# Feed-forward blocks of 512 tokens, with the last 64 tokens of every batch gathered into a ninth block, in a fused attention, Fourier-mixing and feed-forward kernel

## The chip, the cores and the metric

The kernel runs on one core of a Trainium2 chip. The metric is the device time of one execution in microseconds (us), as the median of several runs. TensorE (PE) multiplies, VectorE (DVE), ScalarE (ACT) and GpSimd (POOL) work on elements, and the queue of SyncE (SP) issues nearly all transfers.

## What is computed

The reference, cut to what matters:

```python
# attention: batch 8, heads 8, seq 576, head_dim 64; keys and values averaged in groups of 8 (72 remain)
scores = scale * np.matmul(q, k_p.transpose(0, 1, 3, 2))
attn = softmax(scores)
x = np.matmul(attn, v_p)              # -> (8, 576, 512)
# mixing: the real part of a 2-D Fourier transform over tokens and channels of one batch
u = x + np.real(np.fft.fft(np.fft.fft(x, axis=1), axis=2))
un = (u - mean(u)) / np.sqrt(var(u) + 1e-06)
out = u + np.maximum(un @ w_ch1, 0.0) @ w_ch2   # 512 -> 2048 -> 512
```

All is float32. Each large product is made from three products of rounded numbers (high by high, low by high, high by low).

## The kernel before

A generator `fe(b)` (L247) is the front end of one batch of 576 tokens, and `ffn` (L705) is the feed-forward part of one block of tokens. The program is written as one loop over blocks (L815): each `ffn` yields twice per step, and at each yield (a position, `pos`) `advance` (L790) lets the front ends of later batches take their next stage, and `prep_w` (L178) prepares one of the 34 pieces of the weights where `need(pos)` (L811) asks for it. A scheduler then fixes the order of the instructions of each engine; the engines work through their queues in that order.

**The feed-forward part.** A block of `nb` tokens goes through 16 steps `f` of 128 hidden channels. A step is 12 matmuls into a PSUM tile `g1` (L731: four channel groups times three products, with the centred input as a high part `unh` and a low part `unl`, and the weights as `w1h` and `w1low`), the positive part split into `hh` (ACT, L735) and `hl` (DVE, L736), and 12 matmuls into four PSUM tiles `acc` (L715, with `w2h` and `w2low`), which come one step later. So a step has 24 matmuls, each as wide as the block. After the last step DVE multiplies each `acc` by the tokens' scale `rb` (L745) and adds it to `U` (L746), and SP stores `U` (L748). The low parts of the weights lie in DRAM (`wls`, L92) and are read again at each step (`load_low`, L211) into a ring of seven places (tag `w`).

**The blocks** (`blocks`, L71). Batch 0 goes in halves of 288 tokens, first both halves through steps 0 to 7 and then both through 8 to 15; batches 1 to 6 go in pairs, each pair of 1152 tokens in three blocks of 384; batch 7 goes in two halves of 288. There are 208 steps in all, 64 of 288 columns and 144 of 384.

**The front end of a batch.** For each of four pairs of heads: loads of keys, queries and values, scores (`psS`, L345), softmax, transposes (`psT`, L385), values (`psX`, L432) into the one tile `X`. Then the channel transform (`psA` L547, `psB` L575), whose results are split on ACT and DVE into `A`, `B` and `AB` (L529 to L535), and the token transform (`psQ`, `psP`, L592). This last stage ends so, from batch 2 on: DVE adds `psQ` and `psP` to `U` and `X` (L598, L599, L607, L608); POOL forms sums and differences in four instructions (L624, L625), while DVE, ACT and DVE again make the sum over channels (`s`, L617 to L620); PE averages it (`psM`, L642, L643); DVE subtracts the mean (L644); ACT rounds `unh` in four instructions (L632); DVE and POOL make `unl`, two instructions each (L633). The scale `rb` follows some stages later. Each batch has a slot of 576 columns in `unh`, `unl`, `U` and `rb` (`slot`, L67), even batches the second and odd ones the first; `free` (L753) gives the position from which the next user of a slot may write it. A front end writes `X` only when the one before it has left it, and the products of the front end share two PSUM tiles (tag `fe`).

Of the kernel before, what the change touches and what calls it, by code (L numbers as in the profile page):

```python
# [8 lines left out]
F32 = mybir.dt.float32  # L9
F32R = mybir.dt.float32r  # L10
# [36 lines left out]
UE = [4, 1, 0]  # L47
UL = [3, 3, 2]

AHEAD, LEAD, PACE = 11, 12, 0.65  # L50

THIRD = 18

# [1 line left out]
E0, O0, E1, O1 = 0, 1, 2, 3  # L55
# [23 lines left out]
def raw(ap):  # L79
    return ap.bitcast(F32)  # L80
# [3 lines left out]
def tile_kernel(ctx: ExitStack, tc: tile.TileContext, qt, kt, vm, vr, w1, w2, cad, cbd, mkd, out):  # L84
    nc = tc.nc
    cp = ctx.enter_context(tc.tile_pool(name="cp", bufs=1))
    wk = ctx.enter_context(tc.tile_pool(name="wk", bufs=1))
# [24 lines left out]
    U = cp.tile([P, 4, RING], F32, name="U")  # L112
# [103 lines left out]
    steps = [f for *_, f0, f1 in blocks() for f in range(f0, f1)]  # L216


    turn, behind = [0], {}
# [27 lines left out]
    def fe(b):  # L247
# [6 lines left out]
        def load(g):  # L254

            k = U[:, g, 0:S] if b == 0 else wk.tile([P, S], F32, tag="k", name=f"k{b}_{g}")
            nc.sync.dma_start(k, kt[b, g])
            q = U[:, g, S:RING] if b == 0 else wk.tile([P, S], F32, tag="q", bufs=2, name=f"q{b}_{g}")
            nc.sync.dma_start(q, qt[b, g])
            st["q", g], st["k", g] = q, k.rearrange("p (j w) -> p j w", w=POOLW)  # L260
# [4 lines left out]
            st["v", g] = v.rearrange("p (d w) -> p d w", d=D)  # L265

        def load_rem(gi):
            r = wk.tile([32, D, POOLW], F32, tag="vr", name=f"vr{b}_{gi}")
            nc.sync.dma_start(r, vr[b, gi].rearrange("p (d w) -> p d w", d=D))
            st["r", gi] = r  # L270

        def total(out, src, pool):

# [428 lines left out]

    at = [0]

    def ffn(ro, nb, to, f0, f1):  # L705
        cl = slice(ro, ro + nb)
        acc = [pp.tile([P, 512], F32, tag=f"acc{e}", name=f"acc{to}_{f0}_{e}")[:, 0:nb] for e in range(4)]

        def gemm2(f, hh, hl, wh, wl):
            order = [(x, e) for x in range(3) for e in range(4)]  # L710
            if f == f1 - 1:
                order = [(x, e) for e in range(4) for x in range(3)]
            for x, e in order:
                w, h = ((wh, hh), (wl, hh), (wh, hl))[x]
                nc.tensor.matmul(acc[e], lhsT=w[:, e], rhs=h, start=(f == f0 and x == 0), stop=(f == f1 - 1 and x == 2))  # L715

        prev = None
        for f in range(f0, f1):
# [8 lines left out]
            ps = pp.tile([P, 512], F32, tag="g1", bufs=2, name=f"g1_{to}_{f}")[:, 0:nb]  # L727
            n = 0
            for w, x in ((ah, unh), (ah, unl), (al, unh)):
                for c, ti in enumerate((E0, O0, E1, O1)):  # L730
                    nc.tensor.matmul(ps, lhsT=w[:, c], rhs=x[:, ti, cl], start=(n == 0), stop=(n == 11))  # L731
                    n += 1
            hh = wk.tile([P, 384], F32R, tag="hh", bufs=2, name="hh")[:, 0:nb]
            hl = wk.tile([P, 384], F32R, tag="hl", bufs=2, name="hl")[:, 0:nb]
# [7 lines left out]
        gemm2(f1 - 1, *prev)  # L742
        for e in range(4):
            u = U[:, e, cl]
            nc.vector.tensor_tensor(out=acc[e], in0=acc[e], in1=rb[:, cl], op=ALU.mult)  # L745
            nc.vector.tensor_tensor(out=u, in0=u, in1=acc[e], op=ALU.add)  # L746
# [4 lines left out]
    free = {1: 0, 2: 64, 3: 128, 4: 160, 5: 224, 6: 256, 7: 320}  # L753
# [36 lines left out]
    def advance(pos):  # L790
        for b in sorted(run):
            r = run[b]
            if r[3] is None:

                upto = (pos + 1 - r[2]) * (npre / (free[b] - 1) if b == 2 else 1)
            else:
                upto = r[3] + pos - max(free[b], r[2]) + 1 if pos >= free[b] else 0
            while r[1] < upto:
                said = next(r[0], "end")
                r[1] += 1  # L800
                if said == "U":
# [12 lines left out]
    pos = 0
    for blk in blocks():  # L815
# [116 lines left out]
```

## Time and profile before

| what | value |
|---|---|
| median of 3 runs | 1094.45 us (1093.58 to 1095.3) |
| span of the profiled execution (the page gives no other time of it) | 1094.2 us |
| PE busy | 1050.1 us, 96% |
| DVE, ACT, POOL busy | 611.6, 416.0, 247.3 us |
| feed-forward matmuls (6 groups of 832) | 4992 |
| loads of low weights (2 groups of 208, 256 KB each) | 416 |
| moved by DMA | 175.80 MB |

How to read it: "busy" is time in which an instruction of the engine was running. Matmuls overlap, and the profile models their ends, so the cost of a matmul is read from the distance between starts and not from its duration. A row of the timeline has the start, the time until the last of the merged instructions ends, the engine, the line, the operation, out<-in and the count. PEclk is the share of full clock that PE was granted. The page's 40 slices show PE at nine tenths or more from the tenth slice on, and lower before.

### The profile page before, as it was taken

How to read it: one execution, taken by the hardware profiler on the slowest of the kernel's cores; microseconds unless marked ns; L12 is line 12 of the kernel's file. 1: busy time of each engine (PE TensorE's matmuls, PEld its weight loads, DVE VectorE, ACT ScalarE, POOL GpSimd, SP SyncE). 2: the span in 40 equal slices, each digit the busy share in tenths (PEclk: the TensorE clock that was granted, in tenths of full speed). 3: DMA queues.
4: the chain of work that ended last, by engine and by line, in shares of the span. 5: the costliest groups of instructions: out<-in, count | busy, mean ns of one | idle time of the engine just before them, and what ended most of it. 6: DMA issues, size and time to landing. Idle time of an engine off the chain costs nothing.

```text
span 1094.2 us, 17702 instructions
## 1 busy us (share of the span) xinstructions
PE 1050.1 (96%) x6606; PEld 1017.7 (93%) x6606; DVE 611.6 (56%) x1237; ACT 416.0 (38%) x1102; POOL 247.3 (23%) x249
## 2 busy tenths in 40 slices
PE   8848898999999999999999999999999999999997
PEld 7637887999999999999999999999999999999997
DVE  7686878856376455756377455756467434522222
ACT  6767764443143331443233341443324322311110
POOL 4463356212230032201240121400322101200000
PEclk9968999999999999999999999999999999999999
DMA  7867977565345454445444444445534334346563
GB/s 242 274 204 254 318 250 227 178 199 170 119 122 161 121 162 135 127 140 166 131 120 148 142 151 130 133 125 156 158 108 155 98 98 124 117 128 189 165 186 99
DMA packets 91878, 175.80 MB, mean 161 GB/s; under 512 B 10128, under 2 KB 17296, under 8 KB 91536
## 3 DMA queue, kind: packets, MB, share of 16 engines
q1 hardware_dynamic: 91504, 172.01, 50.7%
q0 software_dynamic: 288, 2.66, 0.7%
q8 instruction: 52, 0.85, 0.3%
q14 instruction: 34, 0.28, 0.1%
HBM read 156.81 MB, written 17.83 MB: 160 GB/s over the span
## 4 chain that ended last, share of the span: by engine, by line
PE 84%; DVE 6%; DMA 4%; ACT 3%; issue 1%; POOL 1%; SPq 0%; DVEq 0%; POOLq 0%; ACTq 0%
PE acc L715 35%; PE g L731 35%; PE psX L432 3%; PE psS L345 3%; PE psA L547 2%; PE psP L592 2%; DMA wst<-in_w 1%; DMA w1low<-w1l 1%; PE psB L575 1%; PE psT L385 1%; DVE wd L199 1%; PE psQ L592 1%; DVE wd L198 1%; DMA k<-in_kt 1%; PE psR L408 1%
## 5 line engine op out<-in xcount | busy, mean ns | idle before, releaser
L735 ACT ACTIVATE hh<-g 128x384 fp32r<-128x384 f32 (+1 forms) x208 | 96.3, 464 | 309.6 <-PE g L731 289.8
L736 DVE SCALAR_TENSOR_TENSOR hl<-g,hh 128x384 fp32r<-128x384 f32 (+1 forms) x208 | 108.6, 522 | 185.0 <-ACT hh L735 183.2
L715 PE MATMUL acc<-hh,w2h 128*128 128x384 f32 (+1 forms) x832 | 190.9, 329 | 0.1
L715 PE MATMUL acc<-hh,w2low 128*128 128x384 f32 (+1 forms) x832 | 187.6, 328 | 1.2 <-DMA w2low<-w2l 1.2
L715 PE MATMUL acc<-hl,w2h 128*128 128x384 f32 (+1 forms) x832 | 182.6, 328 | 0.7 <-DVE hl L736 0.7
L731 PE MATMUL g<-unh,w1low 128*128 128x384 f32 (+1 forms) x832 | 178.7, 329 | 4.5 <-DMA w1low<-w1l 4.4
L731 PE MATMUL g<-unl,w1h 128*128 128x384 f32 (+1 forms) x832 | 178.1, 329 | 0.9 <-DVE unl L633 0.9
L731 PE MATMUL g<-unh,w1h 128*128 128x384 f32 (+1 forms) x832 | 175.4, 327 | 0.1
L731 PEld LDWEIGHTS g<-unh,w1low 128*128 128x128 f32 x832 | 140.8, 190 | 6.2 <-DMA w1low<-w1l 5.8
L715 PEld LDWEIGHTS acc<-hh,w2low 128*128 128x128 f32 x832 | 144.4, 189 | 2.0 <-DMA w2low<-w2l 1.4
L715 PEld LDWEIGHTS acc<-hh,w2h 128*128 128x128 f32 x832 | 143.2, 189 | 2.8 <-ACT rt L372 0.8
L715 PEld LDWEIGHTS acc<-hl,w2h 128*128 128x128 f32 x832 | 141.5, 190 | 1.5 <-DVE hl L736 0.9
L731 PEld LDWEIGHTS g<-unl,w1h 128*128 128x128 f32 x832 | 140.4, 190 | 2.1 <-DVE unl L633 1.3
L731 PEld LDWEIGHTS g<-unh,w1h 128*128 128x128 f32 x832 | 140.4, 190 | 1.5 <-issue 0.8
L364 POOL TENSOR_TENSOR t<-t,sm 128x720 f32<-128x720 f32 x32 | 45.9, 1434 | 286.7 <-DVE sm L363 248.0
L280 POOL TENSOR_TENSOR k<-k 128x288 f32<-128x288 f32 (+1 forms) x56 | 41.0, 732 | 97.6 <-DMA k<-in_kt 84.3
L624 POOL TENSOR_TENSOR U<-X,U 128x576 f32<-128x576 f32 (+1 forms) x14 | 20.0, 1433 | 129.2 <-DVE X L608 129.2
L349 DVE TENSOR_REDUCE mx<-psS 128x6 f32<-128x432 f32 (+1 forms) x64 | 33.1, 526 | 19.6 <-PE psS L345 19.3
L345 PE MATMUL psS<-kpb,q 128*128 128x144 f32 x280 | 42.7, 286 | 1.3 <-ACT w2h L203 0.9
L345 PEld LDWEIGHTS psS<-kpb,q 128*128 128x128 f32 x280 | 39.4, 189 | 1.7 <-ACT w2h L203 1.1
L360 ACT ACTIVATE t<-t 128x720 f32<-128x720 f32 x30 | 24.1, 804 | 37.1 <-DVE t L358 36.8
L745 DVE TENSOR_TENSOR acc<-acc,rb 128x384 f32<-128x384 f32 (+1 forms) x60 | 29.0, 517 | 13.5 <-PE acc L715 13.5
(209 smaller groups left out, 1426.9 us busy)
## 6 DMA issues: line engine op xcount, KB each, us to landing
w1low<-w1l SPq DMA_DIRECT2D x208, 256.0 KB, 2.8
w2low<-w2l SPq DMA_DIRECT2D x208, 256.0 KB, 2.9
wst<-in_w SPq DMA_DIRECT2D x30, 512.0 KB, 4.7
q<-in_qt SPq DMA_DIRECT2D x28, 288.0 KB, 3.1
k<-in_kt SPq DMA_DIRECT2D x28, 288.0 KB, 2.9
v<-in_vm SPq DMA_DIRECT2D x28, 256.0 KB, 3.0
out<-U SPq DMA_DIRECT2D x18, 384.0 KB, 3.6
w1l<-wd SPq DMA_DIRECT2D x16, 256.0 KB, 5.1
```

The costliest lines, as they stand in the source:

```text
L280: nc.gpsimd.tensor_tensor(out=out if n == 1 else src[:, :, 0:n], in0=src[:, :, 0] if n == 1 else src[:, :, 0:n], in1=src[:, :, 1] if n == ...
L345: mm = nc.tensor.matmul(ps[:, c * W2J:(c + 1) * W2J], lhsT=q[:, r0:r0 + P], rhs=kpb[g % 2], start=True, stop=True)
L349: nc.vector.tensor_reduce(out=mx[:, c0:c0 + n], in_=pv, op=ALU.max, axis=AX.X, negate=(b, g) in SM)
L360: nc.scalar.activation(t, t, AF.Exp, scale=1.0 / 64.0)
L364: ins = nc.gpsimd.tensor_tensor(out=t, in0=t, in1=sm.unsqueeze(3).broadcast_to([P, 5, 2, J]), op=ALU.mult)
L432: last = nc.tensor.matmul(ps, lhsT=w, rhs=a, start=(i == 0), stop=(i == len(mm) - 1))
L592: nc.tensor.matmul(ps, lhsT=w, rhs=a, start=(i == 0), stop=(i == 6))
L715: nc.tensor.matmul(acc[e], lhsT=w[:, e], rhs=h, start=(f == f0 and x == 0), stop=(f == f1 - 1 and x == 2))
L731: nc.tensor.matmul(ps, lhsT=w[:, c], rhs=x[:, ti, cl], start=(n == 0), stop=(n == 11))
L735: nc.scalar.activation(hh, ps, AF.Relu)
L736: nc.vector.scalar_tensor_tensor(out=hl, in0=ps, scalar=0.0, in1=raw(hh), op0=ALU.max, op1=ALU.subtract)
L745: nc.vector.tensor_tensor(out=acc[e], in0=acc[e], in1=rb[:, cl], op=ALU.mult)
```

## The change

All eight batches are cut into a first block of 512 tokens, 0 to 511, and a rest of 64. `blocks` gives nine blocks of 512: one for each batch, in its slot, and a ninth that holds the eight rests, in the slot of the even batches. When the front end of a batch has ended, `keep_rest` copies the 64 columns of `unh`, `unl`, `U` and `rb` to DRAM (four DMAs), and before the ninth block `load_rest` reads all rests back (four DMAs, 512 columns each). There are 144 steps in all, each with 24 matmuls of 512 columns; the first step's 12 matmuls into `g1` are cut in columns of 288 and 224. `hh` and `hl` grow to 512 columns. To make room, the left-over rows of values (`vr`) lose their own tile and share the one place of the tile `v`, so that each of the two kinds waits until the other was read. `free` becomes 32 positions per batch, and `PACE` and `LEAD` have the 34 pieces of the weights prepared at one per position (11 ahead) where it was 0.65. The ring of the weights keeps its seven places. The order of the tokens in the output changes, which the host undoes.

```diff
-AHEAD, LEAD, PACE = 11, 12, 0.65
+AHEAD, LEAD, PACE = 11, 8, 1.0
...
-    r = [(slot(0) + h * HS, HS, h * HS, f, f + 8) for f in (0, 8) for h in range(2)]
-    for m in range(3):
-        r += [(i * 384, 384, S + m * RING + i * 384, 0, NFC) for i in range(3)]
-    return r + [(slot(7) + h * HS, HS, 7 * S + h * HS, 0, NFC) for h in range(2)]
+    return [(slot(b % B), b * NB) for b in range(B + 1)]
...
-            r = wk.tile([32, D, POOLW], F32, tag="vr", name=f"vr{b}_{gi}")
+            r = wk.tile([P, POOLW * D], F32, tag="v", name=f"vr{b}_{gi}")[0:32]
...
+            for c0, c1 in ((0, HS), (HS, NB)) if step == 0 else ((0, NB),):
+                n = 0
+                for w, x in ((ah, unh), (ah, unl), (al, unh)):
+                    for c, ti in enumerate((E0, O0, E1, O1)):
+                        nc.tensor.matmul(ps[:, c0:c1], lhsT=w[:, c], rhs=x[:, ti, ro + c0:ro + c1], start=(n == 0), stop=(n == 11))
...
+    def keep_rest(b):
+        cl = slice(slot(b) + NB, slot(b) + S)
+        for t, r in zip((raw(unh), raw(unl), U), rests):
+            nc.sync.dma_start(r[:, :, b], t[:, :, cl])
+        nc.sync.dma_start(rests[3][:, 0, b], rb[:, cl])
...
-    free = {1: 0, 2: 64, 3: 128, 4: 160, 5: 224, 6: 256, 7: 320}
+    free = {b: 2 * NFC * (b - 1) for b in range(1, B)}
...
-        return max(AHEAD + PACE * pos, pos - 16 + LEAD)
+        return max(AHEAD + PACE * pos, pos + LEAD)
```

The scheduler orders the instructions anew. On PE, at the end of the front end of batch 3 (names with a 3 after `ps`; `psS4` belongs to the next batch), before the change:

```order
L731 MATMUL g1_1344_3_4834<-unh_83,w1h_68 128x384
L592 MATMUL psP3_2_4701<-cb_71,A0_3792 128x290 x3
L592 MATMUL psP3_2_4701<-cb_71,A1_3793 128x290 x3
L592 MATMUL psP3_2_4701<-cb_71,AB2_3794 128x290
L731 MATMUL g1_1344_3_4834<-unh_83,w1h_68 128x384 x3
L345 MATMUL psS4_3_0_4759<-kpb1_76,q4_3_4744 128x144 x3
L731 MATMUL g1_1344_3_4834<-unl_84,w1h_68 128x384 x4
L731 MATMUL g1_1344_3_4834<-unh_83,w1low_4711 128x384 x4
L715 MATMUL acc1344_0_0_4603<-hh_4728,w2h_69 128x384
L715 MATMUL acc1344_0_1_4604<-hh_4728,w2h_69 128x384
L715 MATMUL acc1344_0_2_4605<-hh_4728,w2h_69 128x384
L715 MATMUL acc1344_0_3_4606<-hh_4728,w2h_69 128x384
```

There the last product of the token transform (`psP3_2`) is followed by matmuls of the feed-forward block of tokens 1344 on (`g1_1344`, `acc1344`), and the averages `psM3` come 20 rows further down. The same place on PE now:

```order
L594 MATMUL psP3_2_3621<-cb_75,A0_3254 128x290 x3
L594 MATMUL psP3_2_3621<-cb_75,A1_3255 128x290 x3
L594 MATMUL psP3_2_3621<-cb_75,AB2_3256 128x290
L345 MATMUL psS4_3_0_3679<-kpb1_80,q4_3_3664 128x144 x3
L345 MATMUL psS4_3_3_3685<-kpb1_80,q4_3_3664 128x144 x2
L644 MATMUL psM3_3709<-s_3653,avg_78 128x288
L645 MATMUL psM3_3709<-s_3654,avg_78 128x288
L644 MATMUL psM3_3713<-s_3653,avg_78 128x288
L645 MATMUL psM3_3713<-s_3654,avg_78 128x288
L345 MATMUL psS4_2_0_3787<-kpb0_79,q4_2_3746 128x144 x3
L345 MATMUL psS4_2_3_3793<-kpb0_79,q4_2_3746 128x144 x2
L735 MATMUL g1_1536_0_4598<-unh_87,w1h_72 128x512
```

The feed-forward block of tokens 1536 on (`g1_1536`) is the block of batch 3 itself: it reads the `unh` and `unl` that this front end makes. From `psB3_0` to this row no matmul of another feed-forward block is left between the front end's products; in front of each of the blocks of batches 3 to 7 it is so from the first `psQ` on. In front of the block of batch 2, 12 feed-forward matmuls stand between the parts of `psQ2_1`, and in front of that of batch 1, 12 stand behind `psQ1_3`.

On DVE, ahead of the sums that take up `psQ3`, before the change:

```order
L736 SCALAR_TENSOR_TENSOR hl_4566<-g1_960_15_4552,hh_4565 128x384
L535 TENSOR_TENSOR AB2_3794<-psB3_2_3885,AB2_3794 32x256
L745 TENSOR_TENSOR acc960_0_0_4061<-acc960_0_0_4061,rb_82 128x384
L745 TENSOR_TENSOR acc960_0_1_4062<-acc960_0_1_4062,rb_82 128x384
L746 TENSOR_TENSOR U_81<-U_81,acc960_0_0_4061 128x384
L745 TENSOR_TENSOR acc960_0_2_4063<-acc960_0_2_4063,rb_82 128x384
L746 TENSOR_TENSOR U_81<-U_81,acc960_0_1_4062 128x384
L745 TENSOR_TENSOR acc960_0_3_4064<-acc960_0_3_4064,rb_82 128x384
L746 TENSOR_TENSOR U_81<-U_81,acc960_0_2_4063 128x384
L736 SCALAR_TENSOR_TENSOR hl_4625<-g1_1344_0_4611,hh_4624 128x384
L746 TENSOR_TENSOR U_81<-U_81,acc960_0_3_4064 128x384
L598 TENSOR_TENSOR U_81<-X_80,psQ3_1_4628 128x288
```

The split of the channel transform (`AB2`) stood ahead of the eight instructions that empty the four `acc` of the block that had ended. On DVE at the same place now:

```order
L750 TENSOR_TENSOR U_85<-U_85,acc1024_0_3523 128x512
L749 TENSOR_TENSOR acc1024_3_3526<-acc1024_3_3526,rb_86 128x512
L750 TENSOR_TENSOR U_85<-U_85,acc1024_1_3524 128x512
L532 TENSOR_TENSOR B0_3306<-psB3_0_3308,B0_3306 128x256
L750 TENSOR_TENSOR U_85<-U_85,acc1024_2_3525 128x512
L532 TENSOR_TENSOR B1_3307<-psB3_1_3338,B1_3307 128x256
L750 TENSOR_TENSOR U_85<-U_85,acc1024_3_3526 128x512
L537 TENSOR_TENSOR AB2_3256<-psB3_2_3347,AB2_3256 32x256
L600 TENSOR_TENSOR U_85<-X_84,psQ3_1_3548 128x288
L601 TENSOR_TENSOR U_85<-X_84,psQ3_1_3548 128x288
L600 TENSOR_TENSOR U_85<-X_84,psQ3_3_3558 128x288
```

The splits `B0`, `B1` and `AB2`, which `psQ3` reads, stand between and behind the instructions that empty the `acc` of the block of batch 2 (`acc1024`).

More of the change, by code (lines that the diff above doesn't have):

```diff
@@ L29 @@
 RING = 2 * S
+NB = 512
+RM = S - NB
 NAT = {0, 1}
@@ L92, in tile_kernel @@
     wls = [dp.tile([P, NFC, DM], F32, name=f"w{i + 1}l") for i in range(2)]
+    rests = [dp.tile([P, n, B, RM], F32, name=f"rest{i}") for i, n in enumerate((4, 4, 4, 1))]
     whs = [cp.tile([P, 12, DM], F32R, name=f"w{i + 1}h") for i in range(2)]
@@ L214, in load_low @@
         nc.sync.dma_start(raw(t), wls[i][:, steps[n]])
-    steps = [f for *_, f0, f1 in blocks() for f in range(f0, f1)]
+    steps = [f for _ in blocks() for f in range(NFC)]
     turn, behind = [0], {}
@@ L703, in tile_kernel, with ffn @@
     at = [0]
-    def ffn(ro, nb, to, f0, f1):
-        cl = slice(ro, ro + nb)
-        acc = [pp.tile([P, 512], F32, tag=f"acc{e}", name=f"acc{to}_{f0}_{e}")[:, 0:nb] for e in range(4)]
+    def ffn(ro, to):
+        cl = slice(ro, ro + NB)
+        acc = [pp.tile([P, NB], F32, tag=f"acc{e}", name=f"acc{to}_{e}") for e in range(4)]
         def gemm2(f, hh, hl, wh, wl):
             order = [(x, e) for x in range(3) for e in range(4)]
-            if f == f1 - 1:
+            if f == NFC - 1:
                 order = [(x, e) for e in range(4) for x in range(3)]
@@ L714, in gemm2 @@
                 w, h = ((wh, hh), (wl, hh), (wh, hl))[x]
-                nc.tensor.matmul(acc[e], lhsT=w[:, e], rhs=h, start=(f == f0 and x == 0), stop=(f == f1 - 1 and x == 2))
+                nc.tensor.matmul(acc[e], lhsT=w[:, e], rhs=h, start=(f == 0 and x == 0), stop=(f == NFC - 1 and x == 2))
         prev = None
-        for f in range(f0, f1):
+        for f in range(NFC):
             step = at[0]
@@ L726, in ffn @@
             ah, al, bh, bl = [x.rearrange("p (c m) -> p c m", m=P) for x in (high(0, f), lows[0, step], high(1, f), lows[1, step])]
[L727 to L734, printed above, removed]
+            ps = pp.tile([P, NB], F32, tag="g1", bufs=2, name=f"g1_{to}_{f}")
+            for c0, c1 in ((0, HS), (HS, NB)) if step == 0 else ((0, NB),):
[3 more added lines that the diff above has]
+                        nc.tensor.matmul(ps[:, c0:c1], lhsT=w[:, c], rhs=x[:, ti, ro + c0:ro + c1], start=(n == 0), stop=(n == 11))
+                        n += 1
+            hh = wk.tile([P, NB], F32R, tag="hh", bufs=2, name="hh")
+            hl = wk.tile([P, NB], F32R, tag="hl", bufs=2, name="hl")
             nc.scalar.activation(hh, ps, AF.Relu)
@@ L746, in ffn, with load_rest @@
             nc.vector.tensor_tensor(out=u, in0=u, in1=acc[e], op=ALU.add)
-            if f1 == NFC and e % 2:
-                nc.sync.dma_start(out[:, e - 1:e + 1, to:to + nb], U[:, e - 1:e + 1, cl])
+            if e % 2:
+                nc.sync.dma_start(out[:, e - 1:e + 1, to:to + NB], U[:, e - 1:e + 1, cl])
         yield
-    free = {1: 0, 2: 64, 3: 128, 4: 160, 5: 224, 6: 256, 7: 320}
+    def keep_rest(b):
[3 more added lines that the diff above has]
+        nc.sync.dma_start(rests[3][:, 0, b], rb[:, cl])
+    def load_rest(ro):
+        cl = slice(ro, ro + NB)
+        for t, r in zip((raw(unh), raw(unl), U), rests):
+            nc.sync.dma_start(t[:, :, cl], r.rearrange("p n b s -> p n (b s)"))
+        nc.sync.dma_start(rb[:, cl], rests[3].rearrange("p n b s -> p (n b s)"))
+    free = {b: 2 * NFC * (b - 1) for b in range(1, B)}
     npre = 20
@@ L777, in tile_kernel @@
                 pass
+            keep_rest(0)
         if n >= NEXT and n2 < 8:
@@ L780, in tile_kernel @@
             n2 += 1
+    keep_rest(1)
     while n2 < STEPS:
@@ L808, in advance @@
                     del run[b]
+                    keep_rest(b)
                     break
     def need(pos):
-        return max(AHEAD + PACE * pos, pos - 16 + LEAD)
+        return max(AHEAD + PACE * pos, pos + LEAD)
     pos = 0
-    for blk in blocks():
+    for n, blk in enumerate(blocks()):
+        if n == B:
+            load_rest(blk[0])
         for _ in ffn(*blk):
```

17 lines of the change are left out of this document (10 added, 7 removed).

## The prediction

> **What bounds the kernel now.** I read the page first, then the sums of fixed stretches, then the timeline of PE. From the page, the busy shares and the chain of waits by engine:
>
> ```profile
> PE 1050.1 (96%) x6606; PEld 1017.7 (93%) x6606; DVE 611.6 (56%) x1237; ACT 416.0 (38%) x1102; POOL 247.3 (23%) x249
> PE 84%; DVE 6%; DMA 4%; ACT 3%; issue 1%; POOL 1%; SPq 0%; DVEq 0%; POOLq 0%; ACTq 0%
> ```
>
> The stretches of the span (length, then busy time of PE, PEld, DVE, ACT, POOL, the granted clock, the DMA share and GB/s):
>
> ```profile
> 0.00:77.00 77.00, 52.49 (x327) 44.52 (x327) 56.13 (x116) 51.14 (x149) 36.07 (x52) 0.89 0.71 239
> 77.00:210.00 133.00, 119.50 (x755) 106.56 (x754) 103.28 (x199) 86.49 (x222) 64.06 (x62) 0.92 0.78 254
> 210.00:960.00 750.00, 750.00 (x4614) 738.90 (x4613) 423.36 (x859) 261.62 (x696) 147.21 (x136) 1.00 0.45 137
> 960.00:1087.20 127.20, 127.20 (x912) 127.10 (x911) 25.85 (x56) 16.74 (x39) 0.00 (x0) 1.00 0.52 157
> 1087.20:1094.20 7.00, 0.90 (x7) 0.67 (x6) 3.00 (x8) 0.00 (x0) 0.00 (x0) 0.80 0.26 84
> ```
>
> From 210 us on PE never stands still: the front ends run inside the feed-forward blocks, and no wait of theirs is seen. So two things count there: what a matmul costs, and whether PE stays fed. Before 210 us the waits come from the first front ends and from the weights.
>
> **Part 1: wider matmuls.** From PE's timeline, first six steps of 384 columns, then five steps of 288; and the counts from the groups by shape (each stands for one of six equal groups):
>
> ```profile
> 958.58 0.85 PE L731 MATMUL g<-unh,w1h 128*128 128x384 f32 x4
> ...
> 983.79 0.42 PE L731 MATMUL g<-unh,w1h 128*128 128x288 f32 x2
> ```
>
> ```profile
> 1064.09 0.70 PE L731 MATMUL g<-unh,w1h 128*128 128x288 f32 x4
> ...
> 1080.04 0.69 PE L731 MATMUL g<-unh,w1h 128*128 128x288 f32 x4
> ```
>
> ```profile
> L731 PE MATMUL g<-unh,w1h 128*128 128x384 f32 x576 | 128.5, 338 | 0.0
> L731 PE MATMUL g<-unh,w1h 128*128 128x288 f32 x256 | 46.9, 305 | 0.1
> ```
>
> A step is 24 matmuls. 25.21 us over 144 matmuls is 175.1 ns each at 384 columns; 15.95 us over 120 is 132.9 ns at 288. The slope is 42.2 ns over 96 columns, 0.44 ns a column, so 512 columns cost 175.1 + 128 x 0.44 = 231.4 ns. Before: 3456 x 175.1 ns + 1536 x 132.9 ns = 605.1 + 204.1 = 809.3 us. After: 9 x 16 x 24 = 3456 matmuls x 231.4 ns = 799.7 us (the 12 halved ones of the first step add nothing that counts). That is **9.6 us less**. Bounds: if cost were in proportion to columns, 233.5 ns, only 2.3 us less; if the slope is 3% smaller, 229.7 ns, 15.5 us less. [...] I go by the rows.
>
> **Part 2: the front end's end in front of each block.** The quoted order of PE shows the new thing. In front of a batch's block, PE's queue holds only the last stage of that batch's own front end, and the block's first matmul reads the `unh` which that stage makes. Whatever of this chain isn't PE work is now waited for. Its steps, as batch 7 went through them while feed-forward matmuls covered it; DVE first, emptying `acc`, splitting, summing:
>
> ```profile
> 911.70 0.57 DVE L745 TENSOR_TENSOR acc<-acc,rb 128x384 f32<-128x384 f32 x1 [0.94 <-PE acc L715]
> ...
> 915.87 0.42 DVE L535 TENSOR_TENSOR AB<-psB,AB 32x256 fp32r<-32x256 f32 x1
> ...
> 930.43 0.74 DVE L607 TENSOR_TENSOR X<-X,psP 128x574 f32<-128x574 f32 x1
> ...
> 937.67 2.62 DVE L644 TENSOR_TENSOR X<-U,psM 128x1152 f32<-128x1152 f32 x2 [1.96 <-PE psM L643]
> ```
>
> Then POOL and PE (`psB` and `psQ`; `psP` costs the same), and from batch 1 the scores:
>
> ```profile
> 933.41 1.82 POOL L625 TENSOR_TENSOR U<-X,U 128x576 f32<-128x576 f32 x1
> 942.23 2.92 POOL L633 TENSOR_TENSOR unl<-X,unh 128x576 fp32r<-128x576 f32 x2 [7.00 <-ACT unh L632]
> ```
>
> ```profile
> 913.92 0.86 PE L575 MATMUL psB<-ca,f 128*32 128x256 f32 x6
> 919.44 0.97 PE L592 MATMUL psQ<-cb,B 128*128 128x288 f32 x6
> 920.25 0.30 PE L592 MATMUL psQ<-cb,AB 96*128 96x288 f32 x1
> 56.86 1.46 PE L345 MATMUL psS<-kpb,q 128*128 128x144 f32 x10 [0.86 <-ACT w2h L203]
> ```
>
> Time zero is the end of the old block's last matmul.
> - Until `AB2`: 911.70 to 916.29 is 4.6 us for emptying four `acc` and the splits. At 512 columns the eight emptying instructions are about 1.0 us longer together (the tail's rows in Part 4), so 5.6; the first starts some 0.8 us before zero, since `acc0` closes four matmuls before the end. `AB2` is there at 4.8.
> - `psQ` and `psP`: five products of 7 matmuls, 0.94 us each (919.44 to 920.38 for 0.97 and 0.30 overlapping), on two PSUM tiles, each waiting for the DVE sum (0.74 and some) of the one two before. With the last 0.15 of `psQ1`, 4 products and the last sum: about 5.2. The sums are done at 10.0.
> - From there to the centring: 931.2 to 937.67 was 6.5 us, in which POOL ended at 935.2 and the rest was PE's queue. Without other matmuls ahead it is between 4.0 and 6.5; I take 5.5, since the scores of the next batch stand in DVE's queue there: 15.5.
> - Centring to the last `unl`: 937.67 to 945.15 is 7.5 us: 23.0.
>
> In these 23 us PE has 18 `psB` (2.1 us), 35 `psQ` and `psP` (4.7), 10 scores (1.2), 4 averages (0.5) and the first 14 matmuls of the block, which need no last `unl` (14 x 0.231 = 3.2): 11.7 us. It stands still for **11.3 us** (9 to 13.5 with the bounds of the third step and a microsecond for the second). After a wait the clock falls. PE in two waits of the first 110 us, and what was granted behind them:
>
> ```profile
> 58.00:60.60 2.60, 0.33 (x3) 0.11 (x1) 2.60 (x8) 1.18 (x5) 2.60 (x4) 1.00 0.64 151
> 60.60:67.50 6.90, 3.20 (x10) 2.58 (x11) 6.90 (x20) 2.65 (x4) 2.44 (x2) 0.51 0.54 207
> 98.90:101.60 2.70, 0.83 (x7) 0.59 (x6) 1.54 (x4) 2.70 (x12) 0.00 (x0) 1.00 1.00 387
> 101.60:108.40 6.80, 6.80 (x24) 5.13 (x22) 5.04 (x7) 5.49 (x15) 4.12 (x4) 0.50 0.73 235
> ```
>
> Two to three idle microseconds brought 6.8 us at half clock. Between the averages and the block's first matmul PE stands still for some 4 us, so I add 2 us for each block (none to 3.4, all of such a stretch worked at half speed). [...] The rows above fell at shorter waits.
>
> So blocks 3 to 7 cost 13.3 us each. In front of blocks 1 and 2, 12 feed-forward matmuls (12 x 0.231 = 2.8 us) still cover the chain: 10.5 each. Sum: 5 x 13.3 + 2 x 10.5 = **87.5 us more** (bounds 55 to 120).
>
> **Part 3: the start.** Batch 0 now needs the 34 pieces of the weights in 16 long steps, not in 32 short ones spread over two passes. PE reaches step 8 later in feed-forward work than before (8 x 24 x 0.231 = 44 us against 16 x 24 x 0.133 = 51 us for the first use of the second half, but 83 against 74 us for the last piece), so no piece is due clearly earlier, and half as many low parts are read in this time. In 77 to 210 us PE stood still for 13.5 us; I leave that unchanged, -4 to +8. The shared tile `v` puts five loads in a row that were three, and the first sums of `vr` and `v` stand in DVE's queue ahead of batch 0's chain: +1 (0 to 3). In the later blocks a low part is loaded three steps, 16 us, ahead of its use through the seven places, which covers `keep_rest`, `load_rest` (it has the whole eighth block) and waits for `v` in SP's queue; without that cover each would cost a load's 3 us.
>
> **Part 4: the end.** From the timeline of DVE and the list of transfers:
>
> ```profile
> 1087.74 1.56 DVE L745 TENSOR_TENSOR acc<-acc,rb 128x288 f32<-128x288 f32 x4 [1.86 <-PE acc L715]
> 1089.21 1.53 DVE L746 TENSOR_TENSOR U<-U,acc 128x288 f32<-128x288 f32 x4
> ```
>
> ```profile
> wst<-in_w SPq DMA_DIRECT2D x30, 512.0 KB, 4.7
> out<-U SPq DMA_DIRECT2D x8, 288.0 KB, 3.4
> ```
>
> The last eight DVE instructions start 0.37 us apart at 288 columns, 0.46 at 384 (911.70 to 916 holds them and two splits), so about 0.58 at 512: 1.7 us longer. A store of 512 KB lands some 1.1 us later than one of 288 KB (between no difference and the 1.3 us of `wst`). Together **+2.8**.
>
> **Sum**, against the profiled span of 1094.2 us, 0.25 us under the median of the runs, which is nothing: 1094.2 - 9.6 + 87.5 + 1 + 2.8 = **1176 us**.
>
> **Rivals.**
> - *Nothing is exposed*: the chain is as short as PE's own work in it, below 12.5 us. Then 1094.2 - 9.6 + 3.8 = 1088, faster. It decides at 0.8 us of wait for each block ((9.6 - 3.8) / 7). For it: DVE, ACT and POOL are half empty. Against it: the four POOL instructions and the 7.5 us behind the centring are serial whatever else is empty. Chance 0.03.
> - *Half exposed*: without feed-forward work beside them, DVE and POOL run the chain in some 17 us, and the clock holds: 5.5 us a block, 1094.2 - 5.8 + 38.5 = 1127. For it: the trace's durations include contention. Chance 0.15.
> - *The blocks wait inside too*: each front end now starts only when its predecessor has ended, and its first half must keep pace with 16 steps; where the scores' or the values' chain falls behind PE's queue, or the weights of the first block do, some 6 us a block come on top: 1176 + 42 = 1218. For it: DVE works 56% and its latency, not its load, decides. Against it: the front end's products stand about one to a step, as before. Chance 0.14.
> - *The change doesn't do what it says*: PE's order shows the nine blocks. Only the width could bring nothing: 1183, inside the forecast.
>
> **Numbers.** A measurement of this kernel tells about 0.2% (2.2 us) from no change. Forecast, 1138 to 1212 us: 0.67. The range 1135 to 1210 us leaves out most of the rivals' cases. Faster 0.03, same 0.01, slower 0.96.
>
> **What would show it.** In the profile of the changed kernel: starts 231 ns apart in the ninth block; seven dips of PE about 125 us apart, each with ACT's `unh` or POOL's and DVE's `unl` as releaser of the first matmuls and waits of `psQ` and `psP` on DVE ahead; half clock behind each. Wrong if PE's row is still full from 250 us on, if the dips are under 6 us, or if the waits are for DMA.

## The result, and the profile after

| what | before | after |
|---|---|---|
| median of 4 runs | 1094.88 us | 1177.89 us (1176.23 to 1181.31) |
| ratio to before, 95% interval | | 1.0762 (1.0742 to 1.0783): slower |
| span of the profiled execution | 1094.2 us | 1175.1 us |
| forecast | | 1176 us (1135 to 1210) |

The page of the changed kernel: busy shares, then PE's and the clock's rows of the 40 slices (29.4 us each):

```profile
PE 1079.5 (92%) x5082; PEld 876.6 (75%) x5082; DVE 616.1 (52%) x1125; ACT 408.8 (35%) x1038; POOL 250.7 (21%) x249
...
PE   7869999699979999899979997999989996999997
...
PEclk9969999799998999899989998999989998999999
```

PE's row, full from the tenth slice on before, now has a dip each 4 to 5 slices, and under each dip, or in the slice behind it, the clock falls. The stretches, in the columns of the prediction's windows: the start, the first block, the seven changes of block, and for comparison one stretch inside a block and the two last blocks:

```profile
0.00:77.00 77.00, 56.14 (x329) 47.40 (x329) 58.53 (x117) 51.53 (x151) 35.58 (x53) 0.88 0.70 232
77.00:207.50 130.50, 122.44 (x540) 94.70 (x540) 77.38 (x138) 75.39 (x184) 52.83 (x49) 0.94 0.74 234
207.50:232.70 25.20, 15.65 (x60) 12.15 (x59) 21.82 (x40) 7.76 (x19) 9.78 (x11) 0.66 0.27 86
337.80:360.60 22.80, 15.40 (x67) 12.55 (x66) 19.95 (x34) 6.33 (x13) 11.70 (x7) 0.78 0.30 96
360.60:461.00 100.40, 100.40 (x481) 82.31 (x480) 49.71 (x97) 36.03 (x98) 15.75 (x19) 1.00 0.39 113
461.00:487.50 26.50, 18.78 (x91) 15.10 (x90) 22.63 (x38) 7.89 (x17) 11.75 (x8) 0.81 0.26 82
588.00:613.40 25.40, 18.14 (x90) 14.21 (x88) 22.40 (x38) 7.87 (x17) 11.72 (x8) 0.80 0.28 86
714.00:740.10 26.10, 18.44 (x89) 14.74 (x87) 22.34 (x38) 7.79 (x17) 11.64 (x7) 0.80 0.26 84
841.00:866.30 25.30, 17.21 (x86) 13.27 (x85) 22.49 (x38) 7.80 (x17) 11.65 (x7) 0.87 0.26 84
967.00:990.20 23.20, 12.81 (x62) 9.67 (x61) 16.54 (x27) 5.89 (x11) 9.42 (x6) 0.78 0.33 110
990.20:1164.00 173.80, 173.80 (x753) 140.81 (x752) 34.47 (x52) 22.43 (x37) 1.42 (x1) 1.00 0.36 108
```

Inside the blocks PE is full at full clock (granted clock 1.00, 0.2 us idle in all of them together). In the seven changes it is idle for 58.1 us (length less PE's busy time, summed). The clock costs there at most 37.3 us (length times one less the clock). Together 95 us at most.

The change of block in front of batch 3, the place that the chapter on the change shows in order. PE first, then DVE, then POOL:

```profile
460.61 0.39 PE L717 MATMUL acc<-hl,w2h 128*128 128x512 f32 x1
460.84 1.57 PE L577 MATMUL psB<-ca,f 128*128 128x256 f32 x12
...
475.96 0.40 PE L644 MATMUL psM<-s,avg 128*128 128x288 f32 x1 [2.41 <-ACT s L621]
...
477.75 0.29 PE L645 MATMUL psM<-s,avg 128*128 128x288 f32 x1
480.54 2.77 PE L345 MATMUL psS<-kpb,q 128*128 128x144 f32 x10 [2.50 <-DVE X L646]
482.93 2.85 PE L735 MATMUL g<-unh,w1h 128*128 128x512 f32 x7
```

```profile
466.46 0.41 DVE L537 TENSOR_TENSOR AB<-psB,AB 32x256 fp32r<-32x256 f32 x1 [0.67 <-ACT AB L536]
...
472.52 0.15 DVE L610 TENSOR_TENSOR X<-X,psP 128x2 f32<-128x2 f32 x1
...
479.14 2.61 DVE L646 TENSOR_TENSOR X<-U,psM 128x1152 f32<-128x1152 f32 x2
```

```profile
474.47 3.81 POOL L627 TENSOR_TENSOR U<-X,U 128x576 f32<-128x576 f32 x2
...
483.68 3.78 POOL L635 TENSOR_TENSOR unl<-X,unh 128x576 fp32r<-128x576 f32 x2
```

The old block's last matmul ends at 461.0, the last low part at 487.46. Between them PE has the front end's last stage and 14 matmuls of the new block, and its four longest waits are for DVE's split of `B` (1.91 us, ahead of the last `psB`), for ACT's rounded sum `s` (2.41), for DVE's part of it (0.72) and for DVE's centring (2.50).

### The profile page after: what moved, and what is told of

It reads as the page before. It is cut to its first block, busy times and chain, and to the rows that moved or that the text cites. A ratio compares the mean times of both kernels' runs of the same rounds, so it can differ in the third digit from the quotient of the medians.

```text
span 1175.1 us, 14183 instructions
## 1 busy us (share of the span) xinstructions
PE 1079.5 (92%) x5082; PEld 876.6 (75%) x5082; DVE 616.1 (52%) x1125; ACT 408.8 (35%) x1038; POOL 250.7 (21%) x249
## 5 line engine op out<-in xcount | busy, mean ns | idle before, releaser
L740 DVE SCALAR_TENSOR_TENSOR hl<-g,hh 128x512 fp32r<-128x512 f32 x144 | 98.8, 687 | 244.4 <-ACT hh L739 243.2
L739 ACT ACTIVATE hh<-g 128x512 fp32r<-128x512 f32 x144 | 85.8, 596 | 299.6 <-PE g L735 293.5
L735 PE MATMUL g<-unh,w1h 128*128 128x512 f32 (+2 forms) x580 | 170.1, 416 | 6.5 <-ACT unh L634 6.5
L717 PE MATMUL acc<-hh,w2h 128*128 128x512 f32 x576 | 171.0, 399 | 0.0
L735 PE MATMUL g<-unl,w1h 128*128 128x512 f32 (+1 forms) x580 | 167.3, 401 | 2.4 <-DVE unl L635 2.1
L735 PE MATMUL g<-unh,w1low 128*128 128x512 f32 (+1 forms) x580 | 164.9, 400 | 1.7 <-DMA w1low<-w1l 1.7
L717 PE MATMUL acc<-hh,w2low 128*128 128x512 f32 x576 | 164.4, 394 | 0.0
L717 PE MATMUL acc<-hl,w2h 128*128 128x512 f32 x576 | 162.7, 397 | 0.0
L717 PEld LDWEIGHTS acc<-hh,w2low 128*128 128x128 f32 x576 | 107.6, 188 | 22.3
L717 PEld LDWEIGHTS acc<-hh,w2h 128*128 128x128 f32 x576 | 106.4, 189 | 23.7 <-issue 0.4
L345 PE MATMUL psS<-kpb,q 128*128 128x144 f32 x280 | 50.7, 328 | 14.9 <-DVE X L646 12.2
L349 DVE TENSOR_REDUCE mx<-psS 128x6 f32<-128x432 f32 (+1 forms) x64 | 32.3, 522 | 12.2 <-PE psS L345 12.1
L361 DVE TENSOR_REDUCE sm<-t 128x10 f32<-128x720 f32 x30 | 27.0, 900 | 15.5 <-ACT t L360 14.9
```

The costliest lines, as they stand in the source:

```text
L345: mm = nc.tensor.matmul(ps[:, c * W2J:(c + 1) * W2J], lhsT=q[:, r0:r0 + P], rhs=kpb[g % 2], start=True, stop=True)
L349: nc.vector.tensor_reduce(out=mx[:, c0:c0 + n], in_=pv, op=ALU.max, axis=AX.X, negate=(b, g) in SM)
L361: nc.vector.tensor_reduce(out=sm, in_=t, op=ALU.add, axis=AX.X)
L717: nc.tensor.matmul(acc[e], lhsT=w[:, e], rhs=h, start=(f == 0 and x == 0), stop=(f == NFC - 1 and x == 2))
L735: nc.tensor.matmul(ps[:, c0:c1], lhsT=w[:, c], rhs=x[:, ti, ro + c0:ro + c1], start=(n == 0), stop=(n == 11))
```

## Two readings, and what they must explain

Theory 1 is the prediction's: the last stage has nothing beside it in PE's queue, so each change of block costs its 13 to 14 us by itself. Theory 2 looks at the whole front end. The last low parts of a batch's front end, of batch 1 before the change (that of batch 7 ended at 945.15), then of batches 1 and 7 after it:

```profile
199.09 2.91 DVE L633 TENSOR_TENSOR unl<-X,unh 128x288 fp32r<-128x288 f32 x3
```

```profile
230.72 2.01 DVE L635 TENSOR_TENSOR unl<-X,unh 128x288 fp32r<-128x288 f32 x2
...
987.28 2.90 POOL L635 TENSOR_TENSOR unl<-X,unh 128x576 fp32r<-128x576 f32 x2 [4.58 <-ACT unh L634]
```

From 202.0 to 945.15 are 743 us for six batches, 123.9 each; from 232.7 to 990.2 they are 126.2. So the front ends follow one another at nearly the same distance in both kernels. What has changed is what stands beside them: 512 tokens of a batch, no longer 576. By theory 2 the rest is waited for, and a lead gained at one place is carried on. It has two forms: the distance is set by the chip's own chain, or by where the scheduler placed the front end's products in PE's queue.

## The experiments

The diffs show the lines that decide. That of e6 is against the kernel before, the others are against the changed kernel.

**e1: more feed-forward work beside the first front end.** Batch 0 and the preparation of the weights as before the change, batches 1 to 7 in blocks of 512:

```diff
-    return [(slot(b % B), b * NB) for b in range(B + 1)]
+    r = [(slot(0) + h * HS, HS, h * HS, f, f + 8) for f in (0, 8) for h in range(2)]
+    r += [(slot(b), NB, S + (b - 1) * NB, 0, NFC) for b in range(1, B)]
+    return r + [(slot(0), 7 * RM, S + 7 * NB, 0, NFC)]
```

> Batch 0 keeps its four half-blocks of 288 columns (168 us from 77 to 245 us, as before the change); batches 1 to 7 go in blocks of 512, and the seven rests in a last block of 448. Without any wait in front of a block: 1094.2 us, less 6.9 us of matmuls (102.1 + 622.3 + 78.1 against 809.3 us), plus 1.9 us at the end: 1089 us. Theory 1 (each block waits for itself, since the end of a front end has nothing beside it): the wait in front of block 1 is gone, the other six cost 13.7 us each as in the changed kernel: 1171 us. Theory 2 (a front end takes some 125 us beside feed-forward work in both kernels, a block of 512 covers 112 us, and a lead is carried on): the front end of batch 1 is 43 us ahead as before, so the first two or three waits are gone and the others stay: 1128 to 1150 us.

Measured 1154.6 us, ratio 1.0539 (1.0522 to 1.0557). Two stretches of it:

```profile
250.00:440.00 190.00, 190.00 (x927) 156.99 (x926) 97.59 (x186) 60.55 (x163) 35.18 (x38) 1.00 0.40 119
440.00:1000.00 560.00, 522.69 (x2480) 427.15 (x2479) 310.92 (x560) 182.63 (x452) 113.32 (x96) 0.95 0.35 105
```

Not one wait up to 440 us, then 37 us of them. The lead is carried on, which theory 1 doesn't allow (1171). It is also used up faster than theory 2 had it, and the time lies above its range: the last low parts of batches 2 (on POOL) and 3 (on DVE) end 147 us apart here, not 125.

```profile
324.90 2.92 POOL L637 TENSOR_TENSOR unl<-X,unh 128x576 fp32r<-128x576 f32 x2 [2.70 <-ACT unh L636]
...
471.80 2.96 DVE L637 TENSOR_TENSOR unl<-X,unh 128x576 fp32r<-128x576 f32 x2
```

**e2: a block of rests in the middle.**

```diff
+    r = [(slot(b), NB, b * NB, 0, NFC) for b in range(B)]
+    return r[:4] + [(slot(3), 256, B * NB, 0, NFC)] + r[4:] + [(slot(0), 256, B * NB + 256, 0, NFC)]
```

> The changed kernel with the rests of batches 0 to 3 in a block of 256 columns between the blocks of batches 3 and 4, those of 4 to 7 in one of 256 at the end (256 columns cost an estimated 119 ns a matmul, so both together 2.5 us more than one of 512). Theory 1: only the wait in front of block 4 is covered, 13.7 us, and reading the rests in the middle costs some 3 us: 1170 us. Theory 2: the middle block gives the front ends a lead of 46 us, which is used up over the next boundaries: block 4 waits for nothing, block 5 for little, blocks 6 and 7 again as before: 1135 to 1160 us.

Measured 1153.9 us, ratio 1.0532 (1.0506 to 1.0557). Around the middle block, which runs from 590 to 652 us:

```profile
230.00:500.00 270.00, 254.32 (x1204) 208.51 (x1203) 152.22 (x287) 92.56 (x241) 58.33 (x54) 0.95 0.35 105
500.00:840.00 340.00, 339.64 (x1848) 289.32 (x1846) 183.21 (x355) 116.39 (x306) 55.92 (x53) 1.00 0.44 131
```

The waits in front of the blocks of batches 4 and 5 are both gone, and not only the first of them: theory 2 again.

**e3: steps half as long.** Each block of 512 becomes one of 288 and one of 224 columns, with the weights prepared as before the change:

```diff
+    h = [(slot(b) + c, n, b * NB + c) for b in range(B) for c, n in ((0, HS), (HS, NB - HS))]
```

> The changed kernel with each block of 512 cut into 288 and 224 columns, one after the other, each with its own 16 steps (batch 0 in turns of 8 steps), and the ninth into two of 256: the same tokens stand beside each front end, in steps half as long; 91.4 us of matmuls a batch in place of 88.9, 13 us in all more than before the change. Theory 1: the waits in front of the batches stay: 1178 + 22 = 1200 us. Theory 2 with a pace that the chip's own chain sets (125 us a batch whatever stands beside it): the waits shrink by what the matmuls grow, only the last blocks add: 1183 us. Theory 2 with a pace set by the turns that the front end's products wait for in PE's queue: with steps half as long the front end is done before the batch needs it, no waits: 1095 + 13 + 1 = 1109 us.

Measured 1131.6 us, ratio 1.0335 (1.0317 to 1.0353).

```profile
250.00:870.00 620.00, 619.12 (x4972) 609.33 (x4971) 383.72 (x808) 235.38 (x654) 144.93 (x132) 1.00 0.60 180
```

Of the waits 0.9 us are left, although the same 512 tokens stand beside each front end (with 5 us more of matmuls): a batch now has 32 short steps for its front end and not 16 long ones, and with them the front end isn't late. The chip's chain as the limit (1183) falls, and so does theory 1 (1200). Of the 22 us above 1109, some 20 are matmuls of 224 columns, which cost more than the straight line through 288 and 384 gave. Two steps of the trace,

```profile
1011.98 0.61 PE L737 MATMUL g<-unh,w1h 128*128 128x224 f32 x4
...
1017.34 0.61 PE L737 MATMUL g<-unh,w1h 128*128 128x224 f32 x4
```

are 5.36 us for 48 matmuls, 111.7 ns each and not 105; 8 x 16 x 24 of them make 20.6 us.

**e4: the changed kernel with another order on PE.** Each first matmul of step `f` is queued behind the products of the next front end whose latest step is `f` (`V` variance, `T` and `R` transposes, `S` scores, `X` values, `A` and `B` channel transform, `Q1` and `QP` token transform, `M` average):

```diff
+    PULL = {'V': 1, 'T3': 1, 'T2': 1, 'R0': 2, 'S0': 2, 'X3': 3, 'X2': 4, 'S1': 4, 'T0': 5, 'T1': 6, 'R1': 7,
+            'X0': 7, 'X1': 8, 'A1': 9, 'A2': 10, 'B1': 11, 'B2': 11, 'Q1': 12, 'QP': 13, 'M': 14}
...
+                      with ExitStack() as stack:
+                        for mark in pull(step) if n == 0 else ():
+                            stack.enter_context(tc.issue_after(mark.ins))
```

> The changed kernel with one thing added: from block 1 on, the products of the next front end are given a latest step (variance and first transposes step 1, values 3 to 8, channel transform 9 to 11, token transform 12 and 13, average 14), behind which the feed-forward step of that number is queued on PE. No work is added or left out. Pace set by the chip's own chain: PE only waits inside the blocks in place of in front of them: 1172 to 1185 us. Pace set by the order in PE's queue: in the changed kernel the products stand ready for some 40 of 126 us and wait for their turn; placed earlier they are done by step 14, and six waits of 13.7 us go, that in front of block 1 stays: 1178 - 82 = 1096 us.

Measured 1115.6 us, ratio 1.0185 (1.0157 to 1.0213).

```profile
207.00:250.00 43.00, 31.06 (x141) 23.86 (x140) 31.01 (x64) 12.41 (x30) 11.61 (x12) 0.83 0.25 78
250.00:925.00 675.00, 664.79 (x3306) 549.40 (x3305) 383.50 (x745) 245.94 (x638) 147.32 (x136) 1.00 0.37 111
```

62 us less with the same instructions. A front end now comes every 115.7 us (from block to block) where it took 126.2, so the order held it back. The wait in front of block 1 stays (11.9 us idle in the first row), as nothing is placed there. The forecast of 1096 was 20 us too low: 3.7 us a batch remain above the 112.0 us of PE work. The waits show 1.9 of them, in two pieces, the new block's `acc` for the emptying of the old, and the average (total, times, longest); the rest isn't placed:

```profile
PE acc L734 <- DVE U L770: 6.0, 5, 1.2
PE psM L650 <- DVE s L627: 3.7, 5, 0.7
```

**e5: e1 and e4 together**, with eight latest steps moved by one (`V`, `T3`, `T2` to 2, `QP` to 12, and with them `R0`, `S0` to 3, `X3` to 4, `S1` to 5).

> The kernel with batch 0 in half-blocks (e1) and the latest steps of e4 together, from block 1 on, with four of these steps moved by one, so that the variance stands behind the emptying of the sums (step 2) and the token transform ends in step 12. If the order in PE's queue is the cause, no wait in front of a block is left: 1089 us, and the 3.7 us a batch by which e4 still exceeded its matmuls (115.7 us from block to block, 112.0 us of PE work) shrink to 1 or 2 us in five batches: 1092 to 1100 us, about the time before. If a front end could not be made faster than in e1: 1150 us.

Measured 1095.25 us, ratio 1.0008 (0.9992 to 1.0024): the same as before the change.

```profile
250.00:905.00 655.00, 652.45 (x3251) 540.73 (x3250) 368.75 (x712) 232.27 (x601) 143.02 (x132) 1.00 0.38 113
```

With cover for the first front end and the order mended, all of the loss is gone, and no gain of the width can be told. This was the best of the versions; none beats the kernel before.

**e6 and e7: the start.** The shared tile alone, put into the kernel before; and the later preparation of the weights, in the changed kernel:

```diff
-            r = wk.tile([32, D, POOLW], F32, tag="vr", name=f"vr{b}_{gi}")
+            r = wk.tile([P, POOLW * D], F32, tag="v", name=f"vr{b}_{gi}")[0:32]
```

```diff
-AHEAD, LEAD, PACE = 11, 8, 1.0
+AHEAD, LEAD, PACE = 11, 9, 0.65
```

> The kernel before with one part of the change alone: the left-over rows of values lose their own tile and share the one of the values, loaded in the changed order. As the prediction has it, the shared tile costs up to 3 us at the start, +1: 1095.6 us. If it is what holds the first front ends up: 1100 us or more; if the first 250 us do not hang on it: 1094 to 1095 us.

> The changed kernel with the weights' pieces prepared as late as they may be: 0.65 a position and nine ahead in place of one a position and eleven ahead. In the changed kernel PE stood still 11 us less in block 0 than over the same tokens before. If the earlier pieces did that, some 5 to 11 us come back: 1183 to 1189 us. If it was that batch 0 goes through the weights once and in long steps, with half as many reads of low parts, the time stays within 3 us of 1178 us.

e6: 1096.3 us, ratio 1.0020 (1.0005 to 1.0034), so the shared tile, with its changed order of loads, costs about 2 us (0.5 to 3.7). e7: 1176.9 us, ratio 1.0759 (1.0736 to 1.0781) beside 1.0762: the pace of the pieces makes no difference that can be told.

**e8: half of the steps.** The second half of the hidden channels is left out:

```diff
+    return [(slot(b % B), NB, b * NB, 0, NFC // 2) for b in range(B + 1)]
```

> The changed kernel with 8 of the 16 steps in each of the nine blocks (the second half of the hidden channels is left out), and the front ends taken in at two stages a position: 44.4 us of matmuls less in each block. Theory 1 (the exposed end alone): each batch takes 126.5 - 44.4 = 82 us: 1178 - 9 x 44.4 = 778 us. Theory 2, pace set by the chip's own chain: a batch still takes some 125 us: about 1089 us. Theory 2, pace set by the order: what is left is the chain without the 40 us of turns, some 86 us a batch, a little more than theory 1 because the middle of the chain now is waited for as well: 800 to 850 us.

Measured 910.2 us (one run): none of the three. The last low parts of batches 3 and 7:

```profile
406.21 3.34 POOL L635 TENSOR_TENSOR unl<-X,unh 128x576 fp32r<-128x576 f32 x2 [4.59 <-DVE unl L635]
```

```profile
808.82 2.90 POOL L635 TENSOR_TENSOR unl<-X,unh 128x576 fp32r<-128x576 f32 x2 [4.58 <-ACT unh L634]
```

402.2 us for four batches are 100.5 each. With 44 us less of matmuls a front end takes 26 us less, so it is neither a fixed 125 us nor just the block and its exposed end (82). Between these two rows PE was busy for 327.9 us, so it stood still for 18.5 us a batch, where a change of block of the changed kernel has 8.3: the middle of the front end is waited for too. The mean clock from 300 to 800 us was 0.83, so part of what lies above 82 is slower work and not waiting.

**e9 and e10: half of the new order.** `PULL` of e4 without its entries from `A1` on (e9), and with these alone (e10).

> e4 with the latest steps of the first half alone (variance, transposes, scores, values: steps 1 to 8); nothing is said of the channel and token transforms and the average, which cover the last stage. Theory 1 (only the exposed end is to blame): the end stays where it is, 1170 to 1178 us. Theory 2 (the whole front end is too late in PE's order): the rest follows its own chain and comes earlier by itself; PE's order has the average half a step ahead of the end of the block, so what follows it, 9.5 us to the last low part, is covered by some 3 us of the old block and 3 us of the new: 4 to 6 us of wait a batch with the clock in place of 13.7: 1178 - 6 x 8 = 1130 us.

> e4 with the latest steps of the second half alone (channel transform 9 to 11, token transform 12 and 13, average 14). Theory 1: the exposed end is gone, so this is e4 again: 1116 us. Theory 2: the values still come late, the last of them stand right ahead of the channel transform in step 9, and PE waits there for what lies between (sums, rounding, about 8 us, less what stands in PE's queue): 5 to 8 us a batch with the clock: 1178 - 6 x 7 = 1136 us.

e9: 1170.7 us, ratio 1.0697 (1.0680 to 1.0715). e10: 1182.4 us, ratio 1.0794 (1.0770 to 1.0818). So e9 came out as theory 1 said, e10 as neither did, and half of the order brings next to nothing. PE's rows tell why: the first product of the last stage and its last average, of batch 3, in e9:

```profile
438.47 0.39 PE L581 MATMUL psB<-ca,f 128*128 128x256 f32 x2
...
475.47 0.29 PE L649 MATMUL psM<-s,avg 128*128 128x288 f32 x1
475.61 0.29 PE L650 MATMUL psM<-s,avg 128*128 128x288 f32 x1
```

and in e4:

```profile
424.75 0.39 PE L581 MATMUL psB<-ca,f 128*128 128x256 f32 x2
...
454.65 0.29 PE L650 MATMUL psM<-s,avg 128*128 128x288 f32 x1
```

In the changed kernel this stage took 16.9 us (460.84 to 477.75, above), alone on PE. In e9 it began 22 us earlier and took 37.1, with feed-forward work between its products as the scheduler placed it (its groups of products start at 438, 445, 451, 457, 463, 471 and 475 us, some 6 us apart); in e4, with latest steps of its own, it takes 29.9. Nearly all that the first half wins, the second gives back. In e10 the values come late, and PE waits ahead of the channel transform instead:

```profile
PE psA L553 <- ACT f L509: 25.6, 6, 5.0
PE psX L435 <- DVE R L421: 10.8, 7, 2.0
```

**e11 and e12: a shorter chain at the change of block.** e11 makes the last stage of all batches in halves and without rounding the sums; e12 holds the next batch's first scores back until the low parts are done, for a theory 3, that DVE's queue is what PE waits for there (DVE is busy for 22.6 of 26.5 us in front of batch 3).

```diff
-HZ = {0, 1}
+HZ = set(range(8))
-NM = {0, 1}
+NM = set(range(8))
```

```diff
+                with tc.issue_after(behind["low", b - 1].ins) if b > 2 and gi == 0 else ExitStack():
+                    nc.vector.tensor_reduce(out=mx[:, c0:c0 + n], in_=pv, op=ALU.max, axis=AX.X, negate=(b, g) in SM)
```

> The changed kernel with the last stage of all batches made as that of batches 0 and 1 is: sums, average and centring in two halves of 288 columns, the average of unrounded sums (the step by way of ACT and DVE, 1.9 us, falls away). The chain from the last sum to the last low part gets shorter by some 3 to 4 us. By both theories the wait falls with it, since nothing covers this stretch: 6 x 3.5 = 21 us: 1157 us. If instead the wait hangs on DVE's queue, in which the next batch's scores stand, not on this chain: 1170 us or more.

> The changed kernel with the first scores of batches 3 to 7 held back: their maxima are queued on DVE behind the low parts of the batch before, so that five of DVE's instructions (some 3.0 us) stand no longer between the last sums and the centring, and the scores' matmuls no longer between the averages and the new block on PE. Theory 3 (at a change of blocks DVE's queue is what PE waits for: 20 to 23 us of DVE work in 23 to 26 us, and whatever of it is not needed there lengthens the wait): 3 to 5 us less in front of each of five blocks, with the clock: 1178 - 5 x 4 = 1158 us (1150 to 1163). Theory 2 (only the whole length of a front end counts): the scores come some 8 us later, the rest as much later, and the time stays or grows: 1175 to 1185 us.

e11: 1177.0 us, ratio 1.0749 (1.0731 to 1.0767). e12: 1179.9 us, ratio 1.0781 (1.0752 to 1.0810). Neither is faster. e11 came out as was said for a wait on DVE's queue, but e12, which tests that alone, came out as theory 2 said (1175 to 1185), and theory 3 falls. The longest group of waits in e11, and the centring in e12:

```profile
PE psM L640 <- DVE t L358: 11.9, 5, 2.6
```

```profile
474.92 2.62 DVE L650 TENSOR_TENSOR X<-U,psM 128x1152 f32<-128x1152 f32 x2 [2.65 <-POOL U L628]
```

With the rounding gone, the average waits for the scores in DVE's queue; with the scores gone, the centring waits for POOL's sums. Three strands of about one length run side by side there, and taking one away shows the next.

## Why the prediction was right, and where it was not

The forecast is 2 us off, the wait lies at the changes of block, where it was put, and the steps hold in their order; but two terms were off in opposite directions, the changes of block by 8 us and the start by 12, so that a hit within 2 us is luck.

- **Width.** In the ninth block the first groups of two steps stand at

```profile
1102.64 1.10 PE L735 MATMUL g<-unh,w1h 128*128 128x512 f32 x4
...
1108.20 1.10 PE L735 MATMUL g<-unh,w1h 128*128 128x512 f32 x4
```

5.56 us for 24 matmuls, 231.7 ns where 231.4 was forecast. So 3456 x 231.7 = 800.7 us, 8.6 less; forecast 9.6.
- **The chain at a change of block**, in front of batch 3, from the old block's end: `AB2` after 5.9 us (forecast 4.8), the sums done after 11.7 (10.0), centring from 18.1 (15.5), last low part after 26.5 (23.0). The four steps were short by 1.1, 0.6, 1.0 and 0.8 us. In the third, ahead of the centring, the value chosen lay between two bounds, 4.0 and 6.5 us, and the scores in DVE's queue and POOL's sums took the upper one.
- **What PE waited for.** The prediction named `unh`, `unl`, `psQ` and `psP`. Over 232 to 1000 us PE waited longest ahead of the next batch's scores, for DVE's centring (12.2 us), ahead of the averages, for the sums on ACT and DVE (9.3 and 5.3), and ahead of `psB`, for the split of `B` (7.5); `psQ` and `psP` have 4.5 us together, and `unh` 5.1 at one place. The chain is the one foretold, but the waits stand earlier in it.
- **The idle time was less, the clock dearer.** 58 us idle are 8.3 a block (forecast 11.3, in front of blocks 1 and 2 8.5), since work at half clock filled part of the wait (in front of batch 3, six matmuls of `psQ` took 1.64 us from 465.45 on, at a granted clock of 0.50; six took 0.97 at 1.00 in the rows of Part 2); the clock took up to 37 us, 5.3 a block, where 2 were added. Together up to 95 against 87.5.
- **Blocks 1 and 2 were no cheaper.** The change in front of block 1 is the dearest of all: 9.6 us idle and a clock of 0.66, up to 18 us together. That in front of block 2 has up to 12.4 us, about as much as most of the others.
- **The start.** Part 3 left the first block's waits as they were and added 1 us. (Its "later" is a slip: by its own figures, 44 against 51 us, PE reaches step 8 earlier than before.) By the windows (idle, and the clock's loss as above) it was 11 us better: from 33.0 to 30.1 up to 77 us, from 24.1 to 15.9 in the first block. e7 shows that the earlier pieces aren't it, e6 that the shared tile costs 2 us. That the long steps with half as many reads of low parts do it was argued, not shown.
- **The end.** The last emptying:

```profile
1166.02 2.49 DVE L749 TENSOR_TENSOR acc<-acc,rb 128x512 f32<-128x512 f32 x4 [3.47 <-PE acc L717]
1168.42 2.47 DVE L750 TENSOR_TENSOR U<-U,acc 128x512 f32<-128x512 f32 x4
```

0.60 us apart, forecast 0.58. From the first of these rows to the end of the span it is 9.1 us, where 6.5 were: 2.6 more (forecast 2.8). The other terms make -8.6 - 11.1 + 95.4 = 75.7 of the 80.9 us, so another 2.6 us are not placed.
- **The reason behind it.** That nothing stands beside the last stage is true, and it is how the loss shows; it isn't the whole cause. The experiments put it one step back. Beside wide steps, as the scheduler ordered them, a front end takes up to 147 us (e1), while a block of 512 with its share of front end takes 114 to 116 (e4, e5, from last low part to last low part). So it is never done in time, and at the change of block its last stage, which took 37 us beside feed-forward work in e9, is finished alone in 17. The rival "nothing is exposed" failed for that reason too: not the chain, but its place in the queue decides.
- **One group to a step.** PE's rows over a whole batch show the place. Count as one group the front end's products that stand between two runs of ten or more feed-forward matmuls. Where the scheduler alone set the order there is about one group to a step: from last low part to last low part 20 to 24 groups in 24 to 25 steps before the change (batches 2 to 7), 20 in 21 for batch 3 of e1, 22 in 24 for batches 4 and 5 of e2. The changed kernel has 16 steps a batch, so 15 or 16 groups find a place for batches 3 to 6, and what is left comes alone at the end; e4 has 20 groups in the 16 steps. The prediction held this fact ("about one to a step, as before") against its third rival, and did not ask whether 16 steps are enough.

What stays open: why the scheduler places about one group to a step, whatever the width. The runs show that it does, and that the chip allows another order (e4); what it reckoned with they don't show. The pace of `advance` doesn't seem to be it: in e8 it takes twice as many stages a step, and there still are 8 to 10 groups in 8 steps.

## What to carry to other kernels

Work that is moved to the end of a kernel stops covering what ran beside it: ask what each stretch of side work needs for cover, and compare that with what is left, over the whole stretch and not only at its end. Where side work gets one turn to a step, count the steps too: fewer and longer ones are fewer turns. Where a fixed order puts a late chain just ahead of its user, shortening one strand of the chain, or ordering half of it, gave next to nothing here (e9 to e12, 1171 to 1182 us beside 1178); more cover, shorter steps, or an order that brings the whole chain forward did (e1 to e4, 1116 to 1155 us). And the wider matmuls saved 8.6 us of 809.3 here, where the changes of block left PE idle for 58.1.

## What the runs showed of the hardware

The clock fell here also behind stretches in which PE was idle only in part. In the trace of the changed kernel the granted clock changes only on a grid of 3.41 us. Two stretches of 3.4 us ahead of block 2, one after the other:

```profile
338.40:341.80 3.40, 1.58 (x12) 0.76 (x10) 3.40 (x9) 0.00 (x0) 0.00 (x0) 0.98 0.65 231
341.80:345.20 3.40, 3.40 (x14) 3.40 (x15) 2.07 (x5) 0.00 (x0) 0.42 (x1) 0.52 0.40 154
```

PE was busy for 1.58 of 3.4 us, and the next 3.4 us ran at half clock. All 17 falls of the clock in this trace came behind such a stretch with 1.8 us of work or less, and none behind a stretch at full clock with more; two stretches with 1.77 and 1.80 us were not followed by one. Of the 17, 11 lie in the seven changes of block, so that four of these have two, and what follows one is 3.4 to 10.2 us at half clock. The forecast had counted with one fall a block, worth 2 us; the second falls, and the length of what follows them, are why the clock cost more.

On the argument for the rival "half exposed", that the trace's durations include contention: before the change DVE's twelve `unl` instructions of 128x576 took 0.75 to 0.76 us, five of them with POOL idle, but for the two of batch 4 (566.4 and 567.9 us), which took 1.57 and 1.98 beside POOL's work. In front of blocks 2 to 6 of the changed kernel all ten ran beside POOL's work and took 1.35 to 1.46 us: longer there, not shorter.
